# Where w_out turned is decoded, and who sums the first batch's exponentials

## The chip, the cores and the metric

The kernel runs on one core of one Trainium2 chip. The metric is the device time of one execution in microseconds (us). The core has a matrix engine (TensorE, PE in the rows; PEld is its weight load), a vector engine (VectorE, DVE), an activation engine (ScalarE, ACT), a general engine (GpSimd, POOL) and SyncE (SP), which here issues nearly all DMAs. Each engine takes its instructions in one fixed order and waits at the first whose inputs are not there.

## The reference, cut to what matters

```
scores = cap * tanh(q k^T / 8 / cap)              # 4 batches, 12 heads, 448 x 448
attn   = exp(scores - max) / (sum(exp(scores - max)) + 1e-9)
x      = attn v, heads side by side               # 1792 tokens x 768
y      = relu(x w_in)^2 w_out                     # 768 -> 2048 -> 768
route  : the largest logits of y w_gate first, one expert per token, 224 tokens per expert
out    = relu(y w1[e]) w2[e]                      # 8 experts, 768 -> 1024 -> 768
```

The kernel leaves the maximum out (it uses a bound from cap in the small constant), so it needs exp(cap tanh(...)) and, for each query, the sum of these over the 448 keys: the denominator.

## The kernel before, in words

The work is traced in Python and then ordered by a planner: it walks a simulated clock and puts every instruction into its engine's order when its inputs are there in that simulation, by trace position where several are ready. What is traced late can therefore be placed early. From the third batch on the order on TensorE is the traced order (`manual_schedule` for PE); the other engines and all DMA queues stay with the planner.

There are four batches. A batch's attention runs over six pairs of heads (`hp`). For each pair `scores` is called four times (`c` = 0 to 3: three chunks of 128 keys for both heads, and one with the last 64 keys of both), each time matmuls, a tanh and an exponential on ScalarE into a tile p. `pv` multiplies the exponentials with v into U. `norm` makes the denominators in a PSUM tile z, adds the constant (L281), takes the reciprocal (L282), and multiplies U by it into x (L284). U and z share two PSUM buffers ("aux"). `split_rows` then splits each x in two parts, xh and xl (L326, L327).

In batches 1 to 3 the exponentials of a pair are first added up on GpSimd in an SBUF tile z: at `c` = 1 two 128x896 tiles, at `c` = 2 another, at `c` = 3 two halves of 64x448 (L250, L252, L256); then two matmuls with ones (L279) give the denominators. In batch 0 they are not added up: TensorE multiplies ones with every p, six matmuls for the three chunks (L274) and one with a block matrix `duo` for the last (L276).

The expert-free layer has `hidden(b)` (x w_in, L406 to L408) and `output(b)` (L463 to L465). Three merged stretches hold most of it: attention 1 with hidden 0; attention 2 with output 0 and hidden 1; attention 3 with output 1 and hidden 2. `merge` advances the stream that is least far in its budget (118, 44 and 26 units in the last). Weights come as int64 words for batch 0: `decode` loads them into a tile raw (two buffers, L335) and VectorE makes float32 of them in three passes (L339 to L341); the result is stored to DRAM and loaded again by later batches (L360, tile wf, three buffers). Each wf tile is split into wh (L367, ScalarE) and wl (L368, VectorE or GpSimd) ahead of its matmuls.

`gate_decode` does the same with w_out turned (transposed): 24 tiles of 128x512, each a load into raw, three VectorE passes into wt, and a store (L519). They are loaded again (L530) only by `gate_weights`, beside hidden 3. It is traced as a third stream of the last stretch, with 24 yields of one unit.

`issue_after(ins)` puts those instructions of its block that run on the engine of `ins` behind `ins` in that engine's order. Before, `self.mark` is the last traced exponential, a ScalarE instruction; a decode has DMAs on SyncE and passes on VectorE, none on ScalarE.

Of the kernel before, what the change touches and what calls it, by code (L numbers as in the profile page):

```python
# [9 lines left out]
F32 = mybir.dt.float32  # L10
# [69 lines left out]
class Kernel:  # L80
# [5 lines left out]
    def run(self):  # L86
        tc = self.tc
        PS = bass.MemoryType.PSUM
        with tc.tile_pool(name="keep", bufs=1) as self.keep, \
                tc.tile_pool(name="wts", bufs=1) as self.wts, \  # L90
                tc.tile_pool(name="psum", bufs=2, space=PS) as self.psum, \
                tc.tile_pool(name="dram", bufs=1, space=bass.MemoryType.DRAM) as self.dram, \
                ExitStack() as right, ExitStack() as left:
            self.setup()
            self.mp = right.enter_context(tc.tile_pool(name="moe1", bufs=1, side="right"))
            self.gpool = self.mp
            xs = right.enter_context(ExitStack())
            self.xp = xs.enter_context(tc.tile_pool(name="x", bufs=ND, side="right"))
            with tc.tile_pool(name="x32", bufs=ND, side="right") as self.xq:
                with tc.tile_pool(name="rows", bufs=ND + 1, side="right") as self.tp, \  # L100
                        tc.tile_pool(name="attn", bufs=2, side="right") as self.ap:
                    merge([(self.attention(0), 44.0)])
                    self.split_rows(0)
                    merge([(self.hidden(0), 58.0), (self.attention(1), 44.0)])
                    for b in range(2, NB):
                        self.split_rows(b - 1)
                        streams = [(chain(self.output(b - 2), self.hidden(b - 1)), 118.0), (self.attention(b), 44.0)]
                        if b == NB - 1:
                            streams.append((self.gate_decode(), 26.0))
                        with tc.manual_schedule(engines={mybir.EngineType.PE}):  # L110
                            merge(streams)
                self.split_rows(NB - 1)
            self.gp = left.enter_context(tc.tile_pool(name="gate", bufs=1))
            last = left.enter_context(ExitStack())
            self.gpool = last.enter_context(tc.tile_pool(name="last", bufs=1))
            with tc.tile_pool(name="gate_load", bufs=5, side="right") as self.gl:
                with tc.manual_schedule(engines={mybir.EngineType.PE}):
                    merge([(self.hidden(NB - 1), 60.0), (self.gate_weights(), 80.0)])
            xs.close()
            self.tp = right.enter_context(tc.tile_pool(name="rows2", bufs=2, side="right"))  # L120
            self.rp = right.enter_context(tc.tile_pool(name="route", bufs=1, side="right"))
            self.router_setup()

            def room():
                last.close()
                self.ep = left.enter_context(tc.tile_pool(name="expert", bufs=2))

            with tc.manual_schedule(engines={mybir.EngineType.PE}):
                self.second(room)
# [47 lines left out]
    def setup(self):  # L177
        nc, keep = self.nc, self.keep
        capt = keep.tile([128, 1], F32, name="capt")
        nc.sync.dma_start(capt, bass.AP(tensor=self.capv.tensor, offset=self.capv.offset, ap=[[0, 128], [1, 1]]))  # L180
        self.capt = capt
        self.ones = keep.tile([128, DH], F32, name="ones")
        nc.vector.memset(self.ones, 1.0)
        self.duo = keep.tile([128, 128], F32, name="duo")
        nc.vector.memset(self.duo, 0.0)
        for h in (slice(0, 64), slice(64, 128)):
            nc.vector.memset(self.duo[h, h], 1.0)
        self.isc = keep.tile([128, 1], F32, name="isc")
        nc.vector.reciprocal(self.isc, capt)
        nc.vector.tensor_scalar(self.isc, self.isc, DH ** -0.5, None, op0=OP.mult)  # L190
        nab = keep.tile([128, 1], F32, name="nab")
        nc.vector.scalar_tensor_tensor(nab, capt, -1.0, capt, op0=OP.mult, op1=OP.min)
        self.eps = keep.tile([128, 1], F32, name="eps")
        nc.scalar.activation(self.eps, nab, AF.Exp)
        nc.vector.tensor_scalar(self.eps, self.eps, 1e-9, None, op0=OP.mult)
        self.L = keep.tile([128, TC, NE], F32, name="L")
        self.cache = {}
        self.wtile = {}
        self.seq, self.at = [], {}
        for b, m in ((0, "i"), (0, "o"), (1, "i"), (1, "o"), (2, "i"), (3, "i"), (3, "o"), (2, "o")):  # L200
            self.at[b, m] = len(self.seq)
            self.seq += [(b, m, j) for j in range(NF if m == "i" else ND * OB)]
        self.G = {}
        self.loaded = self.ready = 0
        self.x_t = {}
        self.tail = []
        self.exps, self.norms = [], []

    def attention(self, b):

        nc, ap = self.nc, self.ap
        qk, P, vt, zs, U = {}, {}, {}, {}, {}
        adder = nc.gpsimd

        def load(hp):
            qk[hp] = t = ap.tile([128, QK], F32, name="qk", bufs=3)
# [10 lines left out]
        def scores(hp, c):  # L227

            t = qk[hp]
            n = 2 if c < KB else 1  # L230
            k, q = t[:, c * 128:(c + 1) * 128], t[:, QK - S:]
            ps = self.psum.tile([128, 2, 512], F32, name="big")
            if c < KB:
                for s in range(2):
                    rows = slice(s * 64, s * 64 + 64)
                    nc.tensor.matmul(ps[:, s, :S], k[rows], q[rows], start=True, stop=True)  # L236
            else:
                nc.tensor.matmul(ps[:, 0, :S], k, q, start=True, stop=True)
            p = ap.tile([128, n, S], F32, name=f"p{n}", bufs=(2, 5)[n - 1])
            nc.scalar.activation(p, ps[:, :n, :S], AF.Tanh, scale=self.isc)  # L240
            e = nc.scalar.activation(p, p, AF.Exp, scale=self.capt)  # L241
            self.mark = e
            if b == 0:
                self.exps.append(e)
            P[hp, c] = p
            if b == 0:
                return
            if c == 1:
                zs[hp] = z = ap.tile([128, 2, S], F32, name="z", bufs=2)
                adder.tensor_add(z, P[hp, 0], p)  # L250
            elif c == 2:
                adder.tensor_add(zs[hp], zs[hp], p)  # L252
            elif c == KB:
                for s in range(2):
                    half = slice(s * 64, s * 64 + 64)
                    adder.tensor_add(zs[hp][half, s], zs[hp][half, s], p[half, 0])  # L256
# [11 lines left out]

        def norm(hp):
            z = self.psum.tile([128, S], F32, name="aux")  # L270
            if b == 0:
                for c in range(KB):
                    for s in range(2):
                        nc.tensor.matmul(z[s * 64:s * 64 + 64], self.ones, P[hp, c][:, s],  # L274
                                         start=(c == 0), stop=False, skip_group_check=True)
                nc.tensor.matmul(z, self.duo, P[hp, KB][:, 0], start=False, stop=True, skip_group_check=True)  # L276
            else:
                for s in range(2):
                    nc.tensor.matmul(z[s * 64:s * 64 + 64], self.ones, zs[hp][:, s], start=True, stop=True)  # L279
            d = ap.tile([128, S], F32, name="d", bufs=1)  # L280
            (nc.vector.tensor_scalar(d, z, self.eps, None, op0=OP.add) if b == 0 else nc.scalar.activation(d, z, AF.Identity, bias=self.eps))  # L281
            nc.vector.reciprocal(d, d)  # L282
            x = self.xq.tile([128, S], F32, name="x")
            m = nc.vector.tensor_mul(x, U.pop(hp), d)  # L284
            if b == 0:
                self.norms.append(m)
            self.x_t[b, hp] = x

        load(0)
# [222 lines left out]
    def gate_decode(self):  # L512

        for i in range(ND * 4):
            t = self.ap.tile([128, 512], F32, name="wt", bufs=2)
            with self.tc.issue_after(self.mark.ins):
                self.decode(t, self.wot[i], 512)
            self.cache["t", i] = self.dram.tile([128, 512], F32, name=f"wt{i}")
            self.nc.sync.dma_start(self.cache["t", i], t)  # L519
            yield 1.0  # L520
# [440 lines left out]
```

## Time and profile before

| what | value |
|---|---|
| median of 3 runs | 1128.45 us (1128.22 to 1129.28) |
| profiled execution | 1124.67 us, its span 1122.9 us |
| PE busy | 1076.1 us, 96% |
| DVE busy | 655.4 us, 58% |
| ACT busy | 545.9 us, 49% |
| POOL busy | 351.1 us, 31% |
| mean granted TensorE clock | 0.988 of full |

A busy time of PE is the time in which some matmul is in its pipeline, so it is no measure of how dense the matmuls stand. Each slice of the following strips is 28.1 us, a digit is the busy share in tenths:

```profile
PE   7999999999797999999999999999999999999997
DVE  4556999978787743445511245654674664455551
PEclk9999999999899999999999999999899999999999
DMA  8433556566877544322265133344582555766530
```

### The profile page before, as it was taken

What the parts mean: (1) busy time and instruction counts of PE and PEld (TensorE: products, weight loads), DVE (VectorE), ACT (ScalarE), POOL (GpSimd) and SP (SyncE); (2) the same over time, 40 slices, a digit from 0 to 9 for tenths busy, and PEclk for the clock granted to TensorE, in tenths of its full rate; (3) what the DMA queues carried; (4) which work ended last, traced back from release to release, by engine and by line L of the source; (5) the groups of instructions that cost most, each with busy time, mean ns of one, the idle gap of its engine ahead of it and who ended that gap; (6) DMA issues with size and microseconds to landing.
All of it is one profiled execution on the core that took longest, in us unless ns stands there. A gap on an engine that the chain in (4) does not pass through costs nothing.

```text
span 1122.9 us, 16040 instructions
## 1 busy us (share of the span) xinstructions
PE 1076.1 (96%) x5926; PEld 843.7 (75%) x5926; DVE 655.4 (58%) x1103; ACT 545.9 (49%) x843; POOL 351.1 (31%) x245
## 2 busy tenths in 40 slices
PE   7999999999797999999999999999999999999997
PEld 2336555776465877767878888888789899999996
DVE  4556999978787743445511245654674664455551
ACT  5768676444564755576655322222132223445551
POOL 0117776655221032322244344535301102210000
PEclk9999999999899999999999999999899999999999
DMA  8433556566877544322265133344582555766530
GB/s 291 162 107 125 195 189 222 185 229 219 300 244 278 195 120 127 116 79 73 86 228 178 48 92 102 101 103 146 178 282 76 173 196 209 258 230 202 192 111 25
DMA packets 79454, 187.20 MB, mean 167 GB/s; under 512 B 8528, under 2 KB 19312, under 8 KB 79376
## 3 DMA queue, kind: packets, MB, share of 16 engines
q1 hardware_dynamic: 64736, 169.24, 44.8%
q0 software_dynamic: 3424, 11.19, 3.3%
q10 hardware_dynamic: 11216, 5.75, 2.0%
q8 instruction: 46, 0.75, 0.3%
q14 instruction: 32, 0.26, 0.1%
HBM read 156.26 MB, written 29.88 MB: 166 GB/s over the span
## 4 chain that ended last, share of the span: by engine, by line
PE 65%; issue 11%; DVE 11%; DMA 9%; ACT 2%; POOL 1%; SPq 1%; POOLq 0%; DVEq 0%; ACTq 0%
PE acc L463 7%; PE big L886 6%; PE acc L465 6%; PE acc L464 6%; PE acc L848 5%; PE acc L406 5%; PE acc L408 4%; PE acc L407 4%; PE big L236 4%; DMA raw<-w_out_t 4%; PE aux L264 4%; PE aux L662 2%; DMA raw<-w_in 2%; PE acc L855 2%; DVE d L282 1%
## 5 line engine op out<-in xcount | busy, mean ns | idle before, releaser
L367 ACT CAST wh<-wf 128x512 fp32r<-128x512 f32 (+1 forms) x187 | 135.1, 723 | 276.9 <-PE acc L464 107.2
L368 POOL TENSOR_TENSOR wl<-wf,wh 128x512 fp32r<-128x512 f32 (+1 forms) x97 | 157.4, 1626 | 209.4 <-ACT wh L367 202.1
L408 PE MATMUL acc<-xh,wl 128*128 128x448 f32 x384 | 142.7, 372 | 12.6 <-DVE wl L368 12.5
L406 PE MATMUL acc<-xh,wh 128*128 128x448 f32 x384 | 151.0, 394 | 3.2 <-ACT wh L367 3.2
L463 PE MATMUL acc<-g,wh 128*128 128x448 f32 x384 | 150.4, 392 | 0.0
L407 PE MATMUL acc<-xl,wh 128*128 128x448 f32 x384 | 141.9, 370 | 1.1 <-DVE xl L327 1.1
L465 PE MATMUL acc<-g,wl 128*128 128x448 f32 x384 | 140.4, 366 | 1.2 <-DVE wl L368 1.2
L464 PE MATMUL acc<-g,wh 128*128 128x448 f32 x384 | 139.8, 364 | 0.0
L368 DVE TENSOR_TENSOR wl<-wf,wh 128x768 fp32r<-128x768 f32 (+1 forms) x90 | 91.4, 1017 | 81.5 <-ACT wh L367 80.2
L886 PE MATMUL big<-wh,g 128*112 128x384 f32 x512 | 117.8, 342 | 0.0
L240 ACT ACTIVATE p<-big,isc 128x896 f32<-128x896 f32 x96 | 86.0, 908 | 30.1 <-PE big L236 30.1
L406 PEld LDWEIGHTS acc<-xh,wh 128*128 128x128 f32 x384 | 72.8, 190 | 35.5 <-issue 19.4
L408 PEld LDWEIGHTS acc<-xh,wl 128*128 128x128 f32 x384 | 72.9, 190 | 24.4 <-DVE wl L368 14.4
L241 ACT ACTIVATE p<-p,capt 128x896 f32<-128x896 f32 x96 | 89.6, 949 | 1.5
L252 POOL TENSOR_TENSOR z<-z,p 128x896 f32<-128x896 f32 x18 | 38.9, 2164 | 164.2 <-ACT p L241 161.1
L886 PEld LDWEIGHTS big<-wh,g 128*112 128x112 f32 x512 | 86.8, 175 | 0.8
L765 POOL DMA_INDIRECT xg<-x,idx x32 | 34.0, 1062 | 170.7 <-PE acc L784 93.5
L463 PEld LDWEIGHTS acc<-g,wh 128*128 128x128 f32 x384 | 72.4, 189 | 14.3 <-issue 9.6
L282 DVE RECIPROCAL d<-d 128x448 f32<-128x448 f32 x24 | 70.7, 2948 | 19.3 <-ACT d L281 19.2
L407 PEld LDWEIGHTS acc<-xl,wh 128*128 128x128 f32 x384 | 72.9, 190 | 10.3 <-issue 4.0
L236 PE MATMUL big<-qk 64*128 64x448 f32 x288 | 72.6, 592 | 6.9 <-DMA qk<-qk 6.3
L418 DVE TENSOR_TENSOR g<-r,g 128x448 fp32r<-128x448 f32 x58 | 44.6, 769 | 59.2 <-ACT g L417 59.2
(185 smaller groups left out, 1940.1 us busy)
## 6 DMA issues: line engine op xcount, KB each, us to landing
g<-w SPq DMA_DIRECT2D x68, 384.0 KB, 6.1
wf<-wi SPq DMA_DIRECT2D x48, 384.0 KB, 3.5
wf<-wo SPq DMA_DIRECT2D x72, 256.0 KB, 2.7
wf<-w SPq DMA_DIRECT2D x36, 384.0 KB, 3.4
raw<-w_in SPq DMA_DIRECT2D x16, 768.0 KB, 4.9
raw<-w_out SPq DMA_DIRECT2D x24, 512.0 KB, 4.2
raw<-w_out_t SPq DMA_DIRECT2D x24, 512.0 KB, 4.7
wt<-wt SPq DMA_DIRECT2D x48, 256.0 KB, 3.4
```

Of the source, the lines that this page charges most:

```text
L236: nc.tensor.matmul(ps[:, s, :S], k[rows], q[rows], start=True, stop=True)
L240: nc.scalar.activation(p, ps[:, :n, :S], AF.Tanh, scale=self.isc)
L241: e = nc.scalar.activation(p, p, AF.Exp, scale=self.capt)
L367: nc.scalar.copy(wh[:, :w], wf[:, :w])
L368: low.tensor_sub(wl[:, :w], wf[:, :w], wh[:, :w].bitcast(F32))
L406: nc.tensor.matmul(ps, wh[:, d], xh, start=(d == 0), stop=False)
L407: nc.tensor.matmul(ps, wh[:, d], xl, start=False, stop=False)
L408: nc.tensor.matmul(ps, wl[:, d], xh, start=False, stop=(d == ND - 1))
L463: nc.tensor.matmul(ps, a, gh, start=(f == 0), stop=False)
L464: nc.tensor.matmul(ps, a, gl, start=False, stop=False)
L465: nc.tensor.matmul(ps, z, gh, start=False, stop=(f == NF - 1))
L886: nc.tensor.matmul(acc[h][:, s, :DM // 2], l, r[:, s * (DM // 2):(s + 1) * (DM // 2)], start=(j == 0 and first), stop=(j == NF2 - 1 and last))
```

## The change

There are two edits. First, `self.mark` is no longer the last exponential but the last traced product x of a norm in batch 3 (L284, a VectorE instruction); it starts as None, and `gate_decode` yields without work until there is one. Its budget in the merge goes from 26 to 30. Second, in batch 0 the sums of exponentials go the way of the other batches, but on VectorE in place of GpSimd; the matmuls with ones on every p and the matrix `duo` are gone.

```
-                            streams.append((self.gate_decode(), 26.0))
+                            streams.append((self.gate_decode(), 30.0))
...
-        self.duo = keep.tile([128, 128], F32, name="duo")
-        nc.vector.memset(self.duo, 0.0)
-        for h in (slice(0, 64), slice(64, 128)):
-            nc.vector.memset(self.duo[h, h], 1.0)
...
+        self.mark = None
...
-        adder = nc.gpsimd
+        adder = nc.vector if b == 0 else nc.gpsimd
...
-            self.mark = e
             if b == 0:
                 self.exps.append(e)
             P[hp, c] = p
-            if b == 0:
-                return
             if c == 1:
                 zs[hp] = z = ap.tile([128, 2, S], F32, name="z", bufs=2)
                 adder.tensor_add(z, P[hp, 0], p)
...
-            if b == 0:
-                for c in range(KB):
-                    for s in range(2):
-                        nc.tensor.matmul(z[s * 64:s * 64 + 64], self.ones, P[hp, c][:, s],
-                                         start=(c == 0), stop=False, skip_group_check=True)
-                nc.tensor.matmul(z, self.duo, P[hp, KB][:, 0], start=False, stop=True, skip_group_check=True)
-            else:
-                for s in range(2):
-                    nc.tensor.matmul(z[s * 64:s * 64 + 64], self.ones, zs[hp][:, s], start=True, stop=True)
+            for s in range(2):
+                nc.tensor.matmul(z[s * 64:s * 64 + 64], self.ones, zs[hp][:, s], start=True, stop=True)
...
+            if b == NB - 1:
+                self.mark = m
...
+            while self.mark is None:
+                yield 1.0
             with self.tc.issue_after(self.mark.ins):
                 self.decode(t, self.wot[i], 512)
```

## Rows read from the trace of the kernel before

**Rows 1.** Busy time by stage; columns are named in the first line.
```profile
core 0: us, PE busy (x) PEld busy (x) DVE busy (x) ACT busy (x) POOL busy (x), PEclk, DMA share, GB/s
12.99:86.07 73.08, 70.66 (x291) 26.25 (x290) 44.92 (x43) 51.43 (x62) 8.21 (x5) 1.00 0.49 172
93.53:189.42 95.89, 93.79 (x405) 58.13 (x405) 91.78 (x72) 69.04 (x106) 68.17 (x37) 1.00 0.54 190
190.00:275.00 85.00, 82.15 (x380) 58.17 (x381) 72.18 (x69) 41.78 (x62) 50.68 (x31) 1.00 0.61 211
275.00:388.00 113.00, 96.58 (x434) 69.76 (x434) 93.12 (x121) 62.35 (x100) 20.62 (x12) 0.95 0.77 262
388.00:558.00 170.00, 170.00 (x807) 125.96 (x806) 78.73 (x75) 105.20 (x162) 48.06 (x27) 1.00 0.33 100
```

**Rows 2.** What TensorE waited for, 260 to 400 us: total, times, longest.
```profile
PE acc L408 <- DVE wl L368: 12.5, 4, 5.2
PE acc L406 <- ACT wh L367: 3.2, 1, 3.2
```

**Rows 3.** Busy time around the two longest holes, columns as in rows 1.
```profile
281.00:286.00 5.00, 1.23 (x5) 0.48 (x3) 4.13 (x4) 1.32 (x2) 0.00 (x0) 1.00 1.00 353
286.00:293.00 7.00, 3.98 (x11) 3.55 (x12) 4.92 (x7) 4.90 (x7) 1.95 (x1) 0.52 0.90 310
345.70:351.30 5.60, 0.39 (x3) 0.01 (x1) 5.53 (x6) 0.83 (x1) 0.00 (x0) 0.98 0.89 311
351.30:355.00 3.70, 3.70 (x11) 2.56 (x11) 3.70 (x8) 1.68 (x3) 0.00 (x0) 0.57 0.46 134
```

**Rows 4.** What VectorE waited for, 270 to 390 us: total, times, longest.
```profile
DVE wt L339 <- DMA raw<-w_out_t: 19.2, 15, 4.2
```

**Rows 5.** What SyncE's DMA queue waited for in the same stretch.
```profile
SPq L519 <- DVE wt L341: 37.3, 20, 4.5
SPq L360 <- DVE wl L368: 18.6, 10, 5.6
```

**Rows 6.** VectorE by line, 275 to 388 us: count, busy us, mean ns, idle before.
```profile
L340 DVE SCALAR_TENSOR_TENSOR wt<-raw,wt 128x512 int32<-128x512 int32 x24 | 24.5, 1022 | 0.5
L341 DVE SCALAR_TENSOR_TENSOR wt<-raw,wt 128x512 int32<-128x512 int32 x24 | 18.2, 757 | 0.5
L339 DVE TENSOR_SCALAR wt<-raw 128x512 int32<-128x512 int32 x24 | 11.7, 487 | 19.2 <-DMA raw<-w_out_t 19.2
```

**Rows 7.** Tile wt, second pass: duration ns least, median, most; first and last start.
```profile
L340 DVE SCALAR_TENSOR_TENSOR wt<-raw,wt x24: 626/691/2618, 275.6 to 378.7; 128x512 int32<-128x512 int32 x24
```

**Rows 8.** VectorE in order of time: start us, us, line and operation.
```profile
412.27 0.61 DVE L284 TENSOR_TENSOR x<-aux,d 128x448 f32<-128x448 f32 x1
...
544.93 0.61 DVE L284 TENSOR_TENSOR x<-aux,d 128x448 f32<-128x448 f32 x1
...
557.97 1.91 DVE L327 TENSOR_TENSOR xl<-x,xh 128x448 fp32r<-128x448 f32 x1 [0.27 <-ACT xh L326]
```

**Rows 9.** TensorE in order of time, the denominators of two pairs: start us, us.
```profile
74.58 2.42 PE L274 MATMUL aux<-p,ones 128*64 128x448 f32 x12
...
78.95 0.92 PE L276 MATMUL aux<-p,duo 128*128 128x448 f32 x2
...
113.76 0.97 PE L279 MATMUL aux<-z,ones 128*64 128x448 f32 x4
```

**Rows 10.** VectorE by line, 12.99 to 86.07 us, columns as in rows 6.
```profile
L281 DVE TENSOR_SCALAR d<-aux,eps 128x448 f32<-128x448 f32 x6 | 4.1, 680 | 10.8 <-PE aux L276 10.8
L284 DVE TENSOR_TENSOR x<-aux,d 128x448 f32<-128x448 f32 x6 | 3.7, 624 | 0.2
L339 DVE TENSOR_SCALAR wf<-raw 128x768 int32<-128x768 int32 x6 | 3.4, 559 | 19.0 <-DMA raw<-w_in 11.1 <-POOL wl L368 7.9
L368 DVE TENSOR_TENSOR wl<-wf,wh 128x768 fp32r<-128x768 f32 x1 | 1.0, 957 | 2.1 <-ACT wh L367 2.1
```

**Rows 11.** GpSimd by line, 388 to 558 us, columns as in rows 6.
```profile
L252 POOL TENSOR_TENSOR z<-z,p 128x896 f32<-128x896 f32 x6 | 12.7, 2114 | 85.4 <-ACT p L241 85.4
```

## The prediction, made before the changed kernel was run

> **What bounds the kernel now.** I read the busy times by stage first, then what TensorE waited for, then the same question one engine back. The stages are: attention 0 (13 to 86 us), attention 1 with hidden 0 (93 to 189), then the second and third merged stretches, the second cut where the decoding of w_out turned begins (190 to 275, 275 to 388, 388 to 558) [rows 1]. TensorE has work in flight nearly all the time in four of the five; in 275 to 388 it is idle for 113 - 96.58 = 16.4 us. That is the only stage with a hole worth the name, and the last stretch, which holds the same kinds of work, has none.
>
> What ends those holes: wl of VectorE, four times, 12.5 us, and wh of ScalarE, 3.2 us [rows 2]. The two longest lie at 281 to 293 and 345.7 to 351.3 us; behind each the granted clock is at 0.52 and 0.57 of full, so mostly at the lower of the two levels, 1.2 GHz, after TensorE had stood idle [rows 3]. VectorE in turn stood still 15 times, 19.2 us, in front of the first pass of a decode whose load had not landed [rows 4]: wl was queued behind that pass. SyncE stood 37.3 us in front of stores of decoded tiles, and the loads of wf are in the same queue, behind these stores [rows 5]. The DMA share is 0.77 in this stage and 0.33 in the next. So the decoding that only hidden 3 needs runs (first second-pass start 275.6 us, last 378.7 us [rows 7]) where VectorE and the DMAs are fullest. It is traced in the last stretch, but the wait it carries binds ScalarE instructions and it has none, so the planner pulled it forward.
>
> **The change part by part.** *A, the decoding leaves 275 to 388 us.* The new mark is a VectorE instruction, and the three passes are too, so each decode now stands behind a norm of batch 3. These norms end with x at 412.3 to 544.9 us, 26.5 us apart [rows 8]. The two loads that fit the two raw buffers are not bound and will still be issued at about 271 to 275 us; the other 22 and all stores move, on VectorE's and on SyncE's order, past everything of batch 2. What goes: 16.4 us of idle TensorE, and the slow clock: 3.98 x 0.48 + 3.70 x 0.43 = 3.5 us of matmul time [rows 3], together 19.9. What may stay: w_out itself is decoded until about 275 us, and at that load (190 to 275) TensorE idles 2.85 in 85 us, 3.8 in 113; in the last stretch 0 [rows 1]. I take 2.0, between them. A = -17.9. Bounds: -19.9 if nothing stays; -11.2 if the first hole (idle 3.77 + 3.02, clock 1.9, so 8.7 us [rows 3]) belongs to the end of w_out and not to w_out turned.
>
> *B, the decoding enters 388 to 558 us.* By the merge's budgets the first norm of batch 3 is traced when the third stream has spent four empty yields; then 4, 5, 5, 5, 4 tiles follow the first five norms and one the last. VectorE gets 54.4 us (24.5 + 18.2 + 11.7 [rows 6]) on top of 78.73: 133 of 170 us, 78%. The DMA share rises by about what separates the two stages, less the longer time: 0.33 + 0.44 x 113/170 = 0.62 or so. Queued behind a waiting pass on VectorE are the wl of output 1 and hidden 2, which TensorE needs in traced order; behind a waiting store on SyncE the loads of wf. So the old mechanism can come back. The trace has no row of this stage with decoding in it. From below: 0, since TensorE has no idle time there now. From above: 19.9, all of today's cost again. The row nearest to the new load is 190 to 275 us: VectorE 85%, DMA 0.61, and a decode every few microseconds; there TensorE idles 3.4%, which is 5.7 us of 170. I take B = +5.7. The last tile is decoded soon after 545 us; hidden 3, beside which the tiles are read, cannot begin before the last x is split, at 558 to 560 us [rows 8], and this tile is the last of 24 to be read, so I put nothing for it.
>
> The Trainium skill, "SBUF — State Buffer", section "SBUF: two separate sides", says that a VectorE instruction with two SBUF inputs and a GpSimd instruction that reads SBUF exclude each other for their whole length. The trace agrees: the second pass has a median of 691 ns and a longest of 2618 [rows 7], about one GpSimd sum (2114 ns [rows 11]) more. GpSimd is busy 28% of the last stretch against 18% of today's place [rows 1], so by this rule the second pass's stretch, 24.5 - 24 x 0.691 = 7.9 us [rows 6, 7], would become an estimated 12.3, which VectorE's idle time there takes; it speaks against the new place, and for the first rival below.
>
> *C, the sums of batch 0.* TensorE loses per pair 2.42 + 0.92 us and gains 0.97 [rows 9]: 2.37, six times 14.2 us. It is dense there (70.66 of 73.08 us [rows 1]), so that is the most that can come back. VectorE gains, per pair, two sums of 128x896, not in the trace before on VectorE; by wl of 128x768 at 957 ns [rows 10] 0.957 x 896/768 = 1.12 each, and two halves at the 0.624 of a 448-column product [rows 10]: 3.48, six times 20.9 us. (On GpSimd the same sum takes 2.11 [rows 11].) Its idle time in the stage is 73.08 - 44.92 = 28.2 us [rows 1], mostly waits for raw w_in, GpSimd's wl and TensorE's denominators [rows 10]; the last of these get shorter. What is late next is VectorE: 44.92 + 20.9 = 65.8 us of work. Behind it, from 93 to 189 us, it is 95.7% busy, so nothing is caught up later. If it is as full in the first stage as there, the stage takes 65.8/0.957 = 68.8 us, 4.3 less. I take C = -4.3, because that row shows how full this engine gets in this program. Bounds: -14.2 (all of TensorE's time comes back) and +20.9 (each of today's waits is a latency of the chain exponential, sum, denominator, reciprocal, x, and no sum finds room in one). The memsets of `duo` run before the first load lands: nothing.
>
> **The sum.** -17.9 + 5.7 - 4.3 = -16.5 us. The profiled execution took 1124.67 us, so 1108.2 by its own time; the median of the runs is 3.8 us above it, which I carry: 1112.0 us.
>
> **The rivals.** *The hole moves along.* The decodes come in bursts behind each norm, the first two of a burst loaded, the others waiting for their loads with wl and wf behind them. For it: the same VectorE order, the same SyncE order, and VectorE only 4 points less full than at 275 to 388 us (82%). Against it: DMA share 0.62 for 0.77, and 190 to 275 us, where an 85% full VectorE starved TensorE little. Then B = 19.9, the sum -2.3: 1126.2 us.
>
> *The sums lengthen the chain of batch 0 (the slower side).* Every denominator now waits for VectorE, in order, where a decode of w_in or a reciprocal may stand ahead. Price: C = +20.9 at the worst, the sum +8.7: 1137.2 us. It decides from C = +12.2 on, which is 58% of the sums finding no room. For it: of the 28.2 us of idle time some ends with the arrival of data and will stay. Against it: 10.8 us of it waited for the very matmuls that become short (L276, [rows 10]).
>
> *TensorE gets all its time back.* If VectorE fills its waits, C = -14.2 and the sum -26.4: 1102.0 us. For it: TensorE is dense in both first stages. Against it: 65.8 us of VectorE work in 58.9 does not fit unless decodes of w_in go later, where it is full.
>
> *The end of w_out made the first hole.* A = -9.2, the sum -7.8: 1120.6 us. For it: the hole begins 6 us after the last decode of w_out, with the DMAs at 1.00. Against it: the stores and loads of w_out turned are already in that traffic.
>
> **How the numbers follow.** Forecast 0.52; TensorE's full return 0.17; first hole stays 0.10; the hole moves along 0.12; longer chain 0.09. 0.2% (2.3 us) is about what a measurement of this kernel can tell from no change. The forecast's own range is 1105 to 1119. From 1100 to 1127 the range takes in three rivals and leaves out the slower one and the tails, under 2 in 10. Faster: the first three cases, 0.79, and a good third of the moved hole: 0.83. Same: the rest of that: 0.07. Slower: the longer chain and a tail: 0.10.
>
> **What will show it.** Passes into wt start after 412 us or its counterpart, at most five to a norm. In the counterpart of 275 to 388 us the waits for wl fall from 12.5 us to under 3, the clock stays at 2.4 GHz, and the DMA share falls to about 0.4. In the last stretch TensorE idles about 6 us (B), with VectorE near 78%. The x of batch 0's last pair is split about 4 us earlier (C); VectorE then is over 90% busy in that stage. I am wrong if waits for wl of ten or more microseconds stand in the last stretch, or if TensorE waits in batch 0 for denominators.

## The result and the profile after

The changed kernel takes 1100.2 us (median of 4 runs, 1098.67 to 1102.91) against 1128.87 us of the kernel before on the same chip: a ratio of 0.9748 (95% interval 0.9726 to 0.9771), 28.7 us. The profiled execution took 1098.67 us, its span 1096.8 us, 26.1 us less than before; the ledger below is made of these two spans.

Lines have moved: a wf load is L349 now (L360 before), a store of a turned tile L510 (L519), the split xl L316 (L327), wh L356 (L367), wl L357 (L368), the passes L328 to L330 (L339 to L341), reciprocal and x L269 and L271 (L282, L284). Of TensorE's matmuls those of hidden are L395 to L397 (L406 to L408), those of output L452 to L454 (L463 to L465). The stages of the changed kernel, columns as in [rows 1]. The last three are cut at the same matmuls as the last three there (380, 434 and about 805 of them); the second stage of [rows 1] is left out, since TensorE's order is not the same in it:

```profile
12.99:82.00 69.01, 63.61 (x242) 21.82 (x240) 62.53 (x67) 52.92 (x65) 10.15 (x6) 0.98 0.53 182
185.20:269.15 83.95, 82.14 (x380) 58.18 (x381) 71.94 (x70) 41.79 (x62) 50.63 (x31) 1.00 0.62 213
269.15:361.63 92.48, 92.38 (x434) 67.82 (x434) 49.03 (x49) 62.84 (x101) 21.79 (x12) 1.00 0.40 124
361.63:531.63 170.00, 169.59 (x803) 124.93 (x802) 123.25 (x144) 103.56 (x159) 44.99 (x26) 1.00 0.62 207
```

The third line answers to 275 to 388 us: 92.5 us where it took 113, TensorE idle 0.1 us instead of 16.4, the clock at 2.4 GHz throughout, the DMA share 0.40 instead of 0.77. The fourth holds the decoding now: VectorE went from 78.73 to 123.25 us in 170, the DMA share from 0.33 to 0.62, and TensorE still idles only 0.4 us. The decodes did go where the order puts them, the second pass from 387.7 us on, after the first x of batch 3 (385.91); the view of tile wt, columns as in [rows 7]:

```profile
L329 DVE SCALAR_TENSOR_TENSOR wt<-raw,wt x24: 684/690/2516, 387.7 to 521.2; 128x512 int32<-128x512 int32 x24
```

What TensorE waited for in the last stretch (362 to 535 us), and VectorE in the same time:

```profile
PE acc L396 <- DVE xl L316: 1.1, 1, 1.1
PE acc L454 <- DVE wl L357: 0.4, 2, 0.2
```

```profile
DVE wt L328 <- DMA raw<-w_out_t: 23.5, 8, 5.8
```

VectorE stands still in front of loads of w_out turned for longer than before (23.5 us, once 5.8; it was 19.2, once 4.2 [rows 4]), and TensorE does not mind. The 12.5 us of waits for wl that [rows 2] has where the decoding was are gone there, and where it is now they are 0.4, two waits of 0.2.

The ledger, in us from the start of each span (VectorE in order of time):

| event | before | after | gained |
|---|---|---|---|
| last x of batch 0 | 83.61 | 79.62 | 4.0 |
| last x of batch 1 | 197.35 | 192.56 | 4.8 |
| first x of batch 3 | 412.27 | 385.91 | 26.4 |
| last x of batch 3 | 544.93 | 519.51 | 25.4 |
| last split xl | 557.97 | 532.55 | 25.4 |
| end of the span | 1122.9 | 1096.8 | 26.1 |

So the sums of batch 0 gave 4.8 us (C), the freed stretch 26.4 - 4.8 = 21.6 (A), and the last stretch gave back 1.0 (B).

### The profile page after: what moved, and what is told of

It is laid out like the page before. It is cut to its first block, busy times and chain, and to the rows that moved or that the text cites. A ratio compares the mean times of both kernels' runs of the same rounds, so it can differ in the third digit from the quotient of the medians.

```text
span 1096.8 us, 15959 instructions
## 1 busy us (share of the span) xinstructions
PE 1063.3 (97%) x5866; PEld 836.7 (76%) x5866; DVE 676.2 (62%) x1124; ACT 543.8 (50%) x843; POOL 351.0 (32%) x245
## 4 chain that ended last, share of the span: by engine, by line
PE 65%; issue 12%; DVE 10%; DMA 8%; ACT 2%; POOL 1%; SPq 1%; POOLq 0%; DVEq 0%; ACTq 0%
PE big L877 6%; PE acc L395 6%; PE acc L452 6%; PE acc L396 6%; PE acc L397 6%; PE acc L454 5%; PE acc L453 5%; PE acc L839 5%; PE aux L258 3%; PE big L233 3%; DMA raw<-w_out 3%; PE aux L653 2%; DVE wf L329 2%; DVE wf L328 2%; PE acc L846 2%
## 5 line engine op out<-in xcount | busy, mean ns | idle before, releaser
L356 ACT CAST wh<-wf 128x512 fp32r<-128x512 f32 (+1 forms) x187 | 135.2, 723 | 268.5 <-PE acc L453 102.2
L357 POOL TENSOR_TENSOR wl<-wf,wh 128x512 fp32r<-128x512 f32 (+1 forms) x97 | 156.5, 1616 | 206.5 <-ACT wh L356 196.9
L395 PE MATMUL acc<-xh,wh 128*128 128x448 f32 x384 | 148.6, 389 | 2.0 <-ACT r L402 2.0
L452 PE MATMUL acc<-g,wh 128*128 128x448 f32 x384 | 150.4, 392 | 0.0
L454 PE MATMUL acc<-g,wl 128*128 128x448 f32 x384 | 140.4, 366 | 1.2 <-DVE wl L357 1.2
L397 PE MATMUL acc<-xh,wl 128*128 128x448 f32 x384 | 140.4, 366 | 0.1
L357 DVE TENSOR_TENSOR wl<-wf,wh 128x768 fp32r<-128x768 f32 (+1 forms) x90 | 88.0, 979 | 61.1 <-ACT wh L356 60.3
L395 PEld LDWEIGHTS acc<-xh,wh 128*128 128x128 f32 x384 | 72.1, 189 | 35.1 <-issue 15.7
L407 DVE TENSOR_TENSOR g<-r,g 128x448 fp32r<-128x448 f32 x58 | 49.4, 851 | 60.2 <-ACT g L406 57.6
L452 PEld LDWEIGHTS acc<-g,wh 128*128 128x128 f32 x384 | 72.4, 189 | 14.4 <-issue 9.6
L396 PEld LDWEIGHTS acc<-xl,wh 128*128 128x128 f32 x384 | 72.6, 189 | 12.4 <-issue 4.1
L269 DVE RECIPROCAL d<-d 128x448 f32<-128x448 f32 x24 | 70.7, 2948 | 16.6 <-ACT d L268 16.5
L454 PEld LDWEIGHTS acc<-g,wl 128*128 128x128 f32 x384 | 72.0, 187 | 9.4 <-DVE wl L357 2.7
```

Of the source, the lines that this page charges most:

```text
L356: nc.scalar.copy(wh[:, :w], wf[:, :w])
L357: low.tensor_sub(wl[:, :w], wf[:, :w], wh[:, :w].bitcast(F32))
L395: nc.tensor.matmul(ps, wh[:, d], xh, start=(d == 0), stop=False)
L396: nc.tensor.matmul(ps, wh[:, d], xl, start=False, stop=False)
L397: nc.tensor.matmul(ps, wl[:, d], xh, start=False, stop=(d == ND - 1))
L452: nc.tensor.matmul(ps, a, gh, start=(f == 0), stop=False)
```

## The experiments

Each was timed beside the kernel before on the same chip (1129.5 to 1130.3 us there). Differences of 2 to 3 us between two of these kernels mean little; events in the trace are sharper.

**One edit at a time.** First the decoding alone:

```
 # the changed kernel, with batch 0 as it was:
+        adder = nc.gpsimd
+            if b == 0:
+                return
...              (L274 and L276 with duo, as before)
```

> Only the first edit: the decoding of w_out turned behind the norms of batch 3; batch 0 is summed by TensorE as before. Theory (the two edits add up; between the traces the x of batch 0 came 3.5 to 4.8 us earlier, the first norm of batch 3 another 21.6 us, and the last stretch gave 1.0 us back): -20.6 us, so 1107 to 1109 us, no TensorE wait for wl in the second merged stretch. Rival (the edits need each other: the earlier x of batch 0 is what lets w_out finish before hidden 1 starts): the first hole stays, about 8 us less gain, 1115 us or more.

It took 1107.74 us (ratio 0.9812, 0.9792 to 0.9832), 21.9 us less than before. There is no hole in the second merged stretch; first x of batch 3 at 392.76 us, last at 526.28. From the last x of batch 1 (199.10, 1.8 us later than before) on that is a gain of 21.3 us and a loss of 0.9: the same A and B as with both edits. The rival falls.

Then the sums alone:

```
 # the changed kernel, with (and the budget 26 again)
+            self.mark = e
-            if b == NB - 1:
-                self.mark = m
-            while self.mark is None:
-                yield 1.0
```

> Only the second edit: batch 0 summed by VectorE, the decoding of w_out turned where the planner put it before. Theory (VectorE bounds the first 190 us, holes of the second stretch untouched): -4.8 us, about 1123.5 us, with 12 to 18 us of TensorE waits for wl and wh left in the second stretch. Rival (TensorE's whole 14.2 us come back and the rest of the gain was this edit's): 1114 us or less. Rival 2 (the holes depend on how the plan falls and change by several us either way): 1118 to 1129 with another pattern of waits.

1123.59 us (0.9954, 0.9936 to 0.9973), 6.0 us less. The last x of batch 1 is at 192.06, so 5.3 us earlier; the holes are there (11.1 us of waits for wl, 3.0 for wh). The edits add up: 21.9 + 6.0 = 27.9 of 28.7 us.

**Is it the order, or the place in the trace?**

```
             while self.mark is None:
                 yield 1.0
-            with self.tc.issue_after(self.mark.ins):
-                self.decode(t, self.wot[i], 512)
+            self.decode(t, self.wot[i], 512)
```

> As the changed kernel, but without the order behind the norm: the decodes are only traced later (after batch 3's first norm). Theory (the planner pulls them forward to where raw becomes free): passes into wt start at about 262 to 270 us, the holes come back, about 1120 us, as with the sums alone. Rival (trace position alone is enough): 1100 us, passes from about 386 us.

1123.78 us (0.9936, 0.9910 to 0.9963). The second pass runs from 269.9 to 373.9 us, and TensorE waits 12.8 us for wl again. Without the order the planner pulls the decodes to where it had them; the later place in the trace does nothing.

**Is it the place, or the pace?** The decisive run leaves the decodes in the last stretch, but puts all behind its first norm:

```
-            if b == NB - 1:
+            if b == NB - 1 and hp == 0:
                 self.mark = m
```

> As the changed kernel, but every decode stands behind the first norm of batch 3 only, so all 24 can run from about 386 us on, as dense as the two raw buffers allow (one in about 4.4 us, as at 275 to 388 us before). Theory (the place decides: in the last stretch TensorE has split weights in reserve, which the end of w_out does not leave at 275 us): within 3 us of the changed kernel, 1098 to 1104 us, TensorE waits for wl under 3 us. Rival (the pace decides: at most five decodes to a norm): the old density brings the old holes, 8 us or more, 1109 us or more.

1117.36 us (0.9899, 0.9870 to 0.9927): 17 us of the gain are gone. The first x of batch 3 is where it was (385.44), the last 17.7 us later (537.19). My theory, that the last stretch has more in reserve, fell. TensorE's and VectorE's waits, 362 to 535 us:

```profile
PE acc L454 <- DVE wl L357: 9.3, 3, 4.7
PE acc L397 <- DVE wl L357: 3.1, 1, 3.1
```

```profile
DVE wt L328 <- DMA raw<-w_out_t: 27.1, 14, 4.6
```

The same window in stages of busy time, the burst first, the changed kernel second:

```profile
362.00:535.00 173.00, 160.65 (x728) 115.49 (x727) 118.98 (x134) 92.56 (x138) 44.26 (x24) 0.96 0.60 193
```

```profile
362.00:535.00 173.00, 171.47 (x810) 126.35 (x809) 126.35 (x147) 105.13 (x161) 47.26 (x27) 1.00 0.61 203
```

VectorE is less busy in the burst (118.98 us), the DMA share is the same (0.60 and 0.61), and TensorE loses 11 us and some clock. So neither VectorE's load nor the traffic of the stretch as a whole made the holes. That holds in 386 to 500 us too, where all the decodes of the burst run: VectorE is busy 85.23 us there, 89.05 in the changed kernel, at a DMA share of 0.74 and 0.69. One of the holes, on VectorE, on ScalarE and on TensorE, start and duration:

```profile
410.63 0.69 DVE L330 SCALAR_TENSOR_TENSOR wt<-raw,wt 128x512 int32<-128x512 int32 x1
414.33 0.43 DVE L328 TENSOR_SCALAR wt<-raw 128x512 int32<-128x512 int32 x1 [3.01 <-DMA raw<-w_out_t]
414.80 0.69 DVE L329 SCALAR_TENSOR_TENSOR wt<-raw,wt 128x512 int32<-128x512 int32 x1
415.52 0.69 DVE L330 SCALAR_TENSOR_TENSOR wt<-raw,wt 128x512 int32<-128x512 int32 x1
416.13 2.94 DVE L269 RECIPROCAL d<-d 128x448 f32<-128x448 f32 x1
418.99 0.63 DVE L357 TENSOR_TENSOR wl<-wf,wh 128x512 fp32r<-128x512 f32 x1
```

```profile
409.12 0.62 ACT L356 CAST wh<-wf 128x512 fp32r<-128x512 f32 x1 [0.54 <-PE acc L453]
```

```profile
419.68 0.74 PE L454 MATMUL acc<-g,wl 128*128 128x448 f32 x1 [4.68 <-DVE wl L357]
```

wh is there at 409.7 us (the n-th wh and the n-th wl belong to one tile), and its wl begins only at 419.0: VectorE has finished a decode, stood 3.0 us before the first pass of the next, done 1.8 of its passes and a reciprocal of 2.9. TensorE has work until 415.0 us and then stands 4.7.

**Pace, or the reciprocal between?** In the changed kernel no decode stands ahead of a reciprocal unless it is late; that could have been what matters. This run spreads the decodes one by one, without regard to norms (the budget is 26 again):

```
-            if b == NB - 1:
-                self.mark = m
...
+        s = low.tensor_sub(wl[:, :w], wf[:, :w], wh[:, :w].bitcast(F32))
+        if self.last_stretch and low is nc.vector:      # set in the last merged stretch
+            self.mark = s
```

> As the changed kernel, but each decode stands behind the last traced split of a weight on VectorE (wl) in place of a norm, so the 24 are spread one by one over the last stretch, about one in 6 us. In the burst run the three long holes were a wl behind a pass waiting for its load; two of them had a reciprocal between as well (3.0 us of waiting, 1.8 of passes, 2.9 of reciprocal). Theory 1 (what counts is that the decodes leave VectorE room in between): 1098 to 1104 us. Theory 2 (what counts is that no decode stands ahead of a reciprocal, which the order behind the norms sees to): holes of 3 us or more come back at some of the six norms, 1108 us or more.

1102.23 us (0.9770, 0.9733 to 0.9807), as the changed kernel. The last stretch, from first to last x of batch 3, takes 132.66 us, where the changed kernel takes 133.60, the burst 151.75 and the kernel before, without any decode, 132.66. VectorE's waits for the loads shrink too:

```profile
DVE wt L328 <- DMA raw<-w_out_t: 3.0, 2, 1.6
```

TensorE has no wait for wl in this stretch at all, where the changed kernel has two of 0.2 us. So it is not the reciprocal between: 24 decodes are free at one in 6.5 us or in groups of five with a pause, and cost 18 us in one run, at one in 4.7. The pace is not the whole of it, as the run with three loads below shows.

**Which queue?** In the burst both VectorE's order and SyncE's can be the one that starves TensorE. This run, the burst otherwise, takes w_out turned off SyncE:

```
-        nc.sync.dma_start(r[:, :w], src)
+        (q or nc.sync).dma_start(r[:, :w], src)         # q=nc.gpsimd for w_out turned
...
-            self.nc.sync.dma_start(self.cache["t", i], t)
+            self.nc.gpsimd.dma_start(self.cache["t", i], t)
```

> As the burst run (all decodes behind the first norm of batch 3), but the loads and stores of w_out turned are issued by GpSimd, not by SyncE, so no load of wf stands behind them. If SyncE's order made the holes (wf late behind a store that waits for a pass): 1098 to 1104 us. If VectorE's order made them (wl behind a pass that waits for its load), or the traffic: 1112 us or more, the same waits for wl.

1119.17 us (0.9907, 0.9878 to 0.9936), so SyncE's order alone is not it. But the result is mixed. In the last stretch waits for wl halve (6.9 us, 12.4 in the burst), and from first to last x of batch 3 it takes 144.4 us, 7.3 less than the burst; 5.6 us are lost before it (first x at 391.02), where a wl on GpSimd is 4.4 us late, behind two of these loads for which GpSimd stood 5.8 and 2.5 us. By its last x (535.43) the run is 1.8 us ahead of the burst; its longer time comes after that. About two fifths of the burst's 18 us may thus be SyncE's; that is read from one execution.

The other queue, the burst again with the loads of w_out turned three deep in place of two:

```
+            r = self.ap.tile([128, 512], I64, name="rt", bufs=1) if i % 3 == 2 else None
             with self.tc.issue_after(self.mark.ins):        # first norm of batch 3 only
-                self.decode(t, self.wot[i], 512)
+                self.decode(t, self.wot[i], 512, r)
```

> As the burst run, but every third decode has a raw buffer of its own, so three loads of w_out turned can be under way in place of two. If VectorE's order made the holes, its waits for these loads fall from 27 to 10 us or less and the holes at least halve: 1101 to 1109 us. If the traffic made them, more loads at once make it worse: 1117 us or more. If SyncE's order made them: 1112 to 1118 us, as a store still stands ahead of a wf load.

1108.24 us (0.9806, 0.9765 to 0.9846), inside the window of VectorE's order. TensorE's waits for wl are 4.8 us, the stretch takes 140.25 us, and VectorE waits half as long as in the burst (13.0 us; 10 or less was expected). It waits under the name of the copy in flight that ended last, the store of the turned tile:

```profile
DVE wt L328 <- DMA wt<-wt: 13.0, 11, 2.5
```

The number of decodes is the burst's, and they follow each other faster still, one in 3.9 us (386.8 to 475.5), yet they cost 6.7 us where the burst costs 18. So a close pace alone does not make the holes; what goes with them is VectorE standing before loads again and again with no pause between (the changed kernel stands 23.5 us, in groups, at a cost of 1). This run does not single VectorE's order out: SyncE's waits in front of the stores of turned tiles fall too, from 56.0 to 39.8 us (384 to 535 us). But the queue run leaves 10.8 of the burst's 18 us with SyncE's order out of the way, so VectorE standing before a load with wl behind it is probably the larger part. In the second stretch, where the kernel before has its holes, no run separates the two; the burst stands for it.

**How many fit?** Every turned tile loaded and decoded twice:

```
             with self.tc.issue_after(self.mark.ins):
                 self.decode(t, self.wot[i], 512)
+                self.decode(t, self.wot[i], 512)
```

> As the changed kernel, but every tile of w_out turned is loaded and decoded twice (48 decodes, 8 to 10 behind a norm). The 24 decodes cost the last stretch about 1 us behind norms and 18 us in one run. Theory (free as long as the decodes of one norm end before the next norm; nine of them at 4.4 us each do not): the stretch fills up as in the burst run, 18 us or more on top, 1117 to 1135 us. Rival (the cost goes with the number of decodes): 1 us more, 1099 to 1104 us.

1155.42 us (1.0216, 1.0188 to 1.0244), 55 us more than the changed kernel, and more than expected. The last stretch takes 168.62 us (35 more), and the decodes run on to 598 us, past its end: the part behind the last split xl takes 22 us more, most of it in one wait of TensorE.

```profile
PE acc L395 <- ACT r L402: 16.5, 1, 16.5
```

```profile
600.60 1.03 ACT L406 CAST g<-r 128x448 fp32r<-128x448 f32 x2 [14.88 <-DMA wt<-wt]
```

Behind that wait ScalarE stands 14.9 us at a g of hidden 3, until a store of a decoded tile has ended, by its time one of the last. So the second 24 decodes cost 57 us by the spans and the first 24 about 1: this is no price per decode. Where between 24 and 48 the cost sets in was not measured.

**What bounds batch 0?** Three runs. GpSimd in place of VectorE:

```
-        adder = nc.vector if b == 0 else nc.gpsimd
+        adder = nc.gpsimd
```

> As the changed kernel, but GpSimd sums batch 0's exponentials too. Theory (VectorE bounds the first 190 us: TensorE got back about 5 of 14.2 us because VectorE had 20.9 us more to do): with VectorE relieved the x of batch 0 comes up to 9 us earlier than in the changed kernel, 1091 to 1096 us. Rival (the chain from the last exponential to the denominator decides): GpSimd takes 2.1 us for a sum and 1.5 for each half where VectorE takes 1.1 and 0.6, so each of six pairs ends about 2.8 us later: 1105 to 1117 us.

1113.67 us (0.9861, 0.9824 to 0.9899). The rival it is: VectorE is 7 us less busy up to 82 us (55.58 for 62.53), yet the last x of batch 0 comes at 94.59, 15 us later. TensorE waits 12.4 us for d, whose reading frees the PSUM buffer, up to 6.1 at once.

The last chunk back on TensorE:

```
-            elif c == KB:
+            elif c == KB and b:
...
+            if b == 0:                                   # after the two matmuls with ones
+                nc.tensor.matmul(z, self.duo, P[hp, KB][:, 0], start=False, stop=True, skip_group_check=True)
```

> As the changed kernel, but in batch 0 the last chunk of each pair (c = 3) is not added on VectorE (two halves, 1.24 us) but multiplied with the block matrix duo on TensorE, as before the change. Per pair VectorE has 1.24 us less, TensorE about 0.8 us more, and the chain from the last exponential to the denominator is about 1 us shorter. If VectorE's load bounds batch 0 (62.5 of 69 us busy): up to 7 us earlier, 1093 to 1097 us. If the chain does: 5 us earlier, 1094 to 1098 us. If TensorE does: 3 to 5 us later, 1103 to 1105 us.

1103.89 us (0.9771, 0.9746 to 0.9797). VectorE is 6.7 us less busy up to 82 us, but the last x of batch 0 is at 80.01 and the first of batch 3 at 386.20, both within 0.4 us of the changed kernel. Of the 4.8 us between the two spans (1101.6 and 1096.8) 4.5 lie after 533 us, in code that the edit does not touch.

And more load on VectorE, whose result nobody reads:

```
+            if b == 0 and c in (1, 2):
+                nc.vector.tensor_add(self.scrap, p, p)   # never read
...              (scrap is a tile of 128x896)
```

> As the changed kernel, but VectorE adds two more pairs of 128x896 tiles per pair of heads in batch 0 into a tile that nobody reads: 12 x 1.1 = 13.2 us more load and no link in the chain. If VectorE's load bounds the first 190 us: 9 to 13 us later, 1109 to 1113 us. If the chain from exponential to x does and VectorE has slack beside it: 0 to 5 us later, 1100 to 1105 us.

1105.29 us (0.9781, 0.9752 to 0.9812). The busy time to 82 us, columns as before:

```profile
12.99:82.00 69.01, 57.56 (x205) 20.24 (x204) 68.53 (x73) 48.53 (x59) 6.89 (x3) 0.90 0.52 179
```

VectorE is full (68.53 of 69.01). The last x of batch 0 comes 9.6 us later for 13.0 us of sums, the last x of batch 1 only 5.0. So VectorE's load counts, but taking some away gains nothing where TensorE gets work for it: what bounds batch 0 was not settled beyond that.

**Both variants together,** the spread decodes and the mixed sums:

```
+            elif c == KB and b:                          # and duo, as in the mixed run
...
+            self.mark = s                                # as in the spread run
```

> The mixed sums together with the decodes spread behind the splits of the last stretch. The spread run and the changed kernel agreed, so the theory is the mixed run's time within 2 us; where the mixed run gains, this gains too.

1102.37 us (0.9749, 0.9717 to 0.9781). By its events it is ahead: its last split xl starts at 530.36 us, 2.2 before the changed kernel's; what follows then takes 7.6 us longer than there. No version measurably beats the changed kernel.

## Why the prediction was right, and where it was off

The direction and the mechanism held: faster, 1112.0 forecast, 1100.2 measured. The size was less good: that is 0.2 us inside the wide range (1100 to 1127) and outside the forecast's own (1105 to 1119). The 11.8 us are made up, but for rounding, of 3.7 in A, 4.7 in B, 0.5 in C, 0.7 behind the last split, and 2.3 because the median lies 1.5 us above the profiled execution and not the 3.8 that I carried. All five fell to the same side. The number is nearest to the third rival's 1102.0, but by chance: that rival had C at -14.2. By its terms:

**A was too small: -17.9 forecast, -21.6 measured (-21.3 with the first edit alone).** The waits of [rows 2, 3, 4, 5] were the right ones, and the hole at 281 us was not the end of w_out: nothing of it stayed without the decoding. For what would stay I kept 2.0 us; it should have been 0. The other 1.7 us lie beyond my bound. By the stages above, the one of 275 to 388 us lost 20.5 us, 16.3 of idle TensorE and 4.2 of busy time where I had 3.5 for the clock; and 1.05 us more went in the stage ahead of it, 83.95 us for 85, where TensorE idles 1.8 us in place of 2.85. I had looked for nothing there.

**B was the term most mis-sized: +5.7 forecast, +1.0 measured.** I took TensorE's idle share from 190 to 275 us, the row with the nearest load of VectorE and the DMAs. The burst shows that load is the wrong measure: with much the same busy times and DMA share B is 18 us or 1, as the decodes come in one run or with pauses. The load itself was a little high too: VectorE is 72.5% busy there, 78% forecast. Both my value and the first rival were possible; which one it would be lay in the order behind the norms, four or five decodes and then a pause, and I had written that order down without drawing the conclusion. The rival's mechanism was real: it is what the burst does.

**C was right in size: -4.3 forecast, -4.8 measured (5.3 alone).** Its reason was only half right. VectorE is 62.53 of 69.01 us busy, 90.6%, and not at the 95.7% at which I let it stop; with scrap sums it goes to 99%. And "nothing is caught up later" was wrong: of 9.6 us lost in batch 0 attention 1 caught up 4.6. Two halves of 64x448 are 0.68 us each in the mean, not 0.62, the long sums 1.09 and 1.07 (1.12 forecast), by these lines of 12.99 to 82 us:

```profile
L250 DVE TENSOR_TENSOR z<-z,p 64x448 f32<-64x448 f32 x12 | 8.1, 679 | 0.1
L244 DVE TENSOR_TENSOR z<-p,p 128x896 f32<-128x896 f32 x6 | 6.5, 1085 | 0.0
L246 DVE TENSOR_TENSOR z<-z,p 128x896 f32<-128x896 f32 x6 | 6.4, 1065 | 0.0
```

The longer chain of the second rival is what GpSimd's sums do (15 us at the last x of batch 0). With VectorE's it shows once: TensorE waits 2.9 us for a denominator's sums, a sign that I had named for being wrong, and it idles 5.4 us of this stage where it idled 2.4. That is probably a part of why so little of TensorE's 14.2 us came back.

```profile
PE aux L266 <- DVE z L250: 2.9, 1, 2.9
```

**The rest.** The last tile was safe: its second pass starts at 521.2 us, the last x is split at 532.55. The run with twice the decodes shows what this step costs when it is not, some 22 us, and that it was not the reading of the tiles that waited, as I had reasoned, but a g of hidden 3. The rule on the shared port in the Trainium skill ("SBUF — State Buffer", section "SBUF: two separate sides") changed nothing in the sum. The second pass is again 0.69 us in the median and 2.5 at the longest; its stretch beyond the median, put at 12.3 us by that rule, is 5.9 (24 passes of 0.937 us in the mean, less 24 of 0.690), and TensorE idles 0.4 us in all.

## What to carry to other kernels

Work that nobody needs soon is not free where the planner finds a gap: on an engine that takes its instructions in order, each piece that can wait for a load puts that wait in front of what stands behind it. Give such work an order behind events that recur, so that a few pieces at a time are followed by a pause, and load its inputs early enough; look at how closely the pieces follow each other and at how long the engine stands before them, not at the busy share of the engine or of the DMAs. And check that the last piece is done before the next stage begins.

## What the runs showed of the hardware that was not expected

The tail from the last split xl to the end of the span is the same code in all these kernels, and it took 564.3 us in the changed kernel, 564.2 in the spread one, 570.7 with the first edit alone and 568.8 with the mixed sums. Around the routing the granted clock mostly differs with it: over 750 to 900 us it is 0.97, 0.93 and 0.94 in the changed kernel, the first edit alone and the mixed sums (the kernel before, at 0.95 over the same part, 775 to 925 us, has 564.9). It need not be a trait of the build: the four executions of the first edit alone took 1106.5 to 1111.7 us, at a mean granted clock of 0.992 to 0.987, and the profiled one is the slowest of them. Some 5 us of a comparison can come from there; the events ahead of it in the trace are free of it. What sets this clock stays open.
